# LSH attention and spatial gating on one core: from one engine in a written order to a list scheduler that orders all five

## The chip, the cores and the metric

The kernel runs on one NeuronCore of a Trainium2 chip. The metric is the device time of one execution in microseconds. The core has five engines with a queue of instructions each: PE (TensorE, matrix products), DVE (VectorE), ACT (ScalarE), POOL (GpSimd) and SP (SyncE, which issues transfers). Each works through its queue in order and waits at an instruction until what it needs is there. The three runs of the kernel before took 862.89, 864.75 and 867.11 us; the median is 864.75.

## The reference

Four batches of eight heads, 768 positions, head size 64. The attention lets a query see only keys that hash to the same bucket; the feed-forward part gates one half of its activations with a product over positions of the other half.

```python
q_bits = (np.einsum('bhsd,dk->bhsk', q, proj) > 0)      # 6 bits a row, k likewise
mask = q_bucket[:, :, :, None] == k_bucket[:, :, None, :]
scores = np.where(mask, scale * np.matmul(q, k.transpose(0, 1, 3, 2)), -1000000000.0)
attn = np.exp(scores - np.max(scores, axis=-1, keepdims=True))
attn = attn / (np.sum(attn, axis=-1, keepdims=True) + 1e-09)
x = np.matmul(attn, v)                                   # heads side by side: (4, 768, 512)

h = np.maximum(x @ w_in, 0.0)                            # 512 -> 1024
u, v = h[..., :512], h[..., 512:]
v_n = (v - mu) / np.sqrt(var + 1e-06)                    # over the 512 features
v_s = np.einsum('ts,bsd->btd', w_spatial, v_n) + b_spatial[None, :, None]
out = (u * v_s) @ w_out
```

## The kernel before, in words

**Tiling.** The 32 heads are handled as 16 pairs (four to a batch), head e = 0 and head e = 1 of a pair on the two halves of the partitions. A pair takes six steps; a step handles 128 rows of both heads against all 768 columns. fp32 numbers are split into a high and a low fp16 part, so most products are three matmuls.

**One step of a pair by queries** (all pairs but 1, 2 and 3). `scores` lets PE write two heads of scores, `sp`, with 16 matmuls (four passes; the last one, over `hk`, adds the bucket mask); DVE (L290) takes the row maximum `nb`; ACT (L291) writes the exponentials `ex`. `turn` lets ACT write the fp16 high part `pp` (L298) and DVE or POOL the low part (L299); SP issues one DMA transpose per head (L301) into `pt`. Three steps later (`LAG`) `weighted` multiplies `pt` with the split values `vp`, 18 matmuls per head, into `pv`. There are two buffers of `sp`, one per head, so the scores of the next step can't be written before the exponentials of this one have been read out.

**One step of a pair by keys** (`KEYS = {1, 2, 3}`, both heads). The scores stand with keys in the rows, so the exponentials need no transpose; they are multiplied in fp32 with `vf` (`weighted_k`, L271, six matmuls). The maxima that this needs ahead are made by `row_max` (extra matmuls `mp` and 72 DVE reductions, L242), `max_row` and `max_move`.

**Around it.** `load_qk` fetches a pair's queries and keys (one buffer, `QKB`). `hash_rows` makes the buckets' bits (PE, DVE) and moves them by eight small transfers into `hk`, from SP (pair 0: half from ACT). `split_qk` makes the fp16 parts `hl` (ACT L191, DVE L192 and L193). `normalize` (DVE, POOL, ACT) divides by the sums; `transpose_x` turns the result into `xt`. `weights_gen` fetches and converts the three weight matrices in 36 jobs. When a batch's four pairs are done, `mlp_units` makes its feed-forward part in units: `v_unit` (`vps`, six), `u_unit` (`ups`, eight), `s_unit` (`sps`, the product over positions, eight), `o_unit` (`ops`, six). `partial_units` does what can be done of the last batch without its last pair (`vpp`, `upp`).

**What sets the order.** PE's order is the order of the program (`manual_schedule(engines={ET.PE})`). In it `steps` goes through the steps; in every step `fill` hands out feed-forward matmuls by a budget of columns (`RATE`, `LRATE`), from one queue of units, a unit wholly before the next. On ACT, DVE, POOL and SP the framework's own scheduler chooses, by the priorities that `at(g, k)` sets and by its own estimate of when things are ready; so an instruction can be put ahead of others that stand earlier in the program.

Of the kernel before, what the change touches and what calls it, by code (L numbers as in the profile page):

```python
# [9 lines left out]
F16 = mybir.dt.float16  # L10
# [9 lines left out]
P = 128  # L20
# [16 lines left out]
def lsh_attention_spatial_gating(  # L37
# [22 lines left out]
    QKB = 1  # L60
    PSB = (2,2,2)
    MT = "m"
    const = ctx.enter_context(tc.tile_pool(name="const", bufs=1))
    ld = ctx.enter_context(tc.tile_pool(name="ld", bufs=2))
    wk = ctx.enter_context(tc.tile_pool(name="wk", bufs=1))
    ps_sc = ctx.enter_context(tc.tile_pool(name="ps_sc", bufs=PSB[0], space=bass.MemoryType.PSUM))
    ps_pv = ctx.enter_context(tc.tile_pool(name="ps_pv", bufs=PSB[1], space=bass.MemoryType.PSUM))
    ps_m = ctx.enter_context(tc.tile_pool(name="ps_m", bufs=PSB[2], space=bass.MemoryType.PSUM))

# [3 lines left out]
    make_identity(nc, ident)  # L73
    ones = const.tile([P, P], F32, name="ones")
    nc.gpsimd.memset(ones, 1.0)
    hc = const.tile([P, 34], F32, name="hc")
    pj, hv = hc[:, 0:32], hc[:, 32:34]

# [4 lines left out]
    for i, t in enumerate(hk):  # L83
        eng = nc.vector if i % 2 else nc.gpsimd
        eng.memset(t, 0.0)
        for e in range(2):
            eng.memset(t[D * e + 32:D * e + D, 0, :], HK)
# [5 lines left out]
    for t in vf:  # L93
        nc.gpsimd.memset(t[:, :, D:D + 1], 1.0)

# [5 lines left out]
    st = {}  # L101

    def weights_gen():
# [4 lines left out]
        jobs = []  # L108
        vi, vo, vs = (x.rearrange("(c p) f -> p c f", p=P) for x in (w_in, w_out, w_sp))
        for src, dst, n, lo, hi, m, f in ((vi, wi, NPAIR, F2, DF, 256, SX), (vi, wi, NPAIR, 0, F2, 256, SX),  # L110
                                          (vs, ws, NT, 0, S, HS, SW), (vo, wo, NF, 0, DM, 256, SX)):
            for c in range(n):
                for h in range(lo, hi, m):
                    jobs.append((src[:, c, h:h + m], [w[:, c, h:h + m] for w in dst], m, f))

        def fetch(i):
            src, _, m, _ = jobs[i]
            t = wk.tile([P, m], src.dtype, tag="raw", bufs=RB, name=f"raw{i}")
            with tc.issue_after(st["tr"]):
                nc.sync.dma_start(out=t, in_=src)  # L120
            return t

        fetched = [fetch(i) for i in range(RB - 1)]
        yield
        nc.sync.dma_start(out=bt, in_=b_sp.partition_broadcast(P))
        for i, (src, dst, m, f) in enumerate(jobs):
            raw = fetched.pop(0)
            if i + RB - 1 < len(jobs):
                fetched.append(fetch(i + RB - 1))
            if src.dtype == F32:  # L130
                w = raw
            else:
                word = raw.bitcast(U32).rearrange("p (n w) -> p w n", w=2)
                high = raw.bitcast(F32).rearrange("p (n w) -> p w n", w=2)[:, 1]
                w = wk.tile([P, m], F32, tag="wf", bufs=2, name=f"w{i}")
                wu = w.bitcast(U32)
                nc.scalar.activation(w, high, AF.Abs)
                nc.vector.tensor_scalar(w, w, TINY, None, op0=ALU.max)
                nc.vector.tensor_scalar(wu, wu, 3, 0x3FFFFFF8, op0=ALU.logical_shift_left, op1=ALU.bitwise_and)
                nc.vector.scalar_tensor_tensor(out=wu, in0=word[:, 1], scalar=0xC0000000, in1=wu, op0=ALU.bitwise_and, op1=ALU.bitwise_or)  # L140
                nc.vector.scalar_tensor_tensor(out=wu, in0=word[:, 0], scalar=29, in1=wu, op0=ALU.logical_shift_right, op1=ALU.bitwise_or)
            nc.scalar.activation(dst[0], w, AF.Copy, scale=f)
            nc.scalar.activation(w, w, AF.Copy, scale=f)
# [20 lines left out]
    def has_keys(p):  # L164
        return p in KEYS

# [541 lines left out]
```

## Time and profile before

The profiled execution took 868.83 us; its span from the first to the last instruction is 867.0 us. Busy time says how long an engine had an instruction under way, not that it worked at full rate.

| | span | busy us | instructions |
|---|---|---|---|
| PE matmul | 867.0 | 692.6 | 6622 |
| PE weight load | | 406.4 | 6622 |
| DVE | | 536.5 | 1011 |
| ACT | | 439.6 | 684 |
| POOL | | 317.7 | 320 |
| DMA, share of 16 engines, q1 | | 57.8% | 104.14 MB in all |

The mean granted clock of TensorE is 0.887. The scores of pair 0 start at 8.26 us, those of pair 4 (the first pair after the ones by keys) at 222.22 us, those of pair 15, the last one, at 741.38 us. So the program has three stretches: the beginning with pairs 0 to 3, the middle with pairs 4 to 14, beside which the feed-forward parts of three batches run, and the end with pair 15 and the last batch's feed-forward part.

### The profile page before, as it was taken

The page shows a single profiled execution, that of the slowest core. Times are in us where ns is not written, and L with a number is a line of the kernel's source. Part 1 is how long each engine was busy: PE and PEld are TensorE (multiplying, and loading weights), DVE is VectorE, ACT ScalarE, POOL GpSimd, SP SyncE. Part 2 cuts the span into 40 slices and gives each one's busy share as a digit, 9 for nine tenths or more (in the row PEclk, how much of TensorE's full clock was granted, in tenths as well). Part 3 has the DMA queues.
Part 4 walks back from the last instruction along what each step waited for, and adds up shares of the span by engine and source line. Part 5 has one row for each costly group of instructions (what it writes and reads, how often), then busy time and mean ns, then how long its engine had stood idle before and what let it go on. Part 6 is the DMA issues. An engine that isn't in the chain of part 4 may idle for free. (4 is left out here: it accounts for less than half of the span.)

```text
span 867.0 us, 16611 instructions
## 1 busy us (share of the span) xinstructions
PE 692.6 (80%) x6622; PEld 406.4 (47%) x6622; DVE 536.5 (62%) x1011; ACT 439.6 (51%) x684; POOL 317.7 (37%) x320
## 2 busy tenths in 40 slices
PE   3645569899588779697768878798879898989897
PEld 1222346577435445364434544454445464655443
DVE  5747583432657898568487959476468866672611
ACT  3324463134457576465556655565456555653511
POOL 5112242202325656318141536125322644350233
PEclk9966768799879889889779979898899899999999
DMA  4552640112357796988687765969496676874000
GB/s 131 116 146 49 165 132 19 37 41 77 65 121 184 150 208 112 190 141 163 119 164 147 133 144 107 198 115 190 89 185 133 110 139 136 150 116 103 2 37 37
DMA packets 290677, 104.14 MB, mean 120 GB/s; under 512 B 277544, under 2 KB 280616, under 8 KB 290600
## 3 DMA queue, kind: packets, MB, share of 16 engines
q1 hardware_dynamic: 290504, 103.05, 57.8%
q8 instruction: 52, 0.85, 0.4%
q14 instruction: 25, 0.20, 0.1%
q10 hardware_dynamic: 96, 0.04, 0.0%
HBM read 27.94 MB, written 6.29 MB: 39 GB/s over the span
## 5 line engine op out<-in xcount | busy, mean ns | idle before, releaser
L291 ACT ACTIVATE ex<-sp,nb 128x768 f32<-128x768 f32 x156 | 137.7, 898 | 120.4 <-DVE ex L290 120.1
L299 DVE TENSOR_TENSOR pp<-ex,pp 128x768 f16<-128x768 f32 x120 | 132.5, 1123 | 77.7 <-ACT pp L298 77.5
L230 PE MATMUL sp<-hl 64*128 64x384 f16 x1152 | 143.3, 375 | 45.7 <-ACT ex L291 43.0
L290 DVE TENSOR_SCALAR_CACHE_REDUCE ex<-sp 128x768 bf16<-128x768 f32 x156 | 142.8, 951 | 36.7 <-PE sp L230 36.4
L230 PEld LDWEIGHTS <-hl 64*128 64x128 f16 x1224 | 66.4, 104 | 153.5 <-issue 121.3
L298 ACT CAST pp<-ex 128x768 f16<-128x768 f32 x156 | 123.6, 832 | 0.1
L299 POOL TENSOR_TENSOR pp<-ex,pp 128x768 f16<-128x768 f32 x36 | 65.9, 1831 | 146.6 <-ACT pp L298 144.1
L314 PE MATMUL pv<-vp,pt 128*128 128x65 f16 x936 | 107.9, 198 | 9.2 <-DVE x L332 8.1
L478 PE MATMUL sps<-ws,vn 128*128 128x384 f16 x576 | 107.5, 336 | 6.4 <-ACT u L463 3.4
L315 PE MATMUL pv<-vp,pt 128*128 128x64 f16 x936 | 107.9, 197 | 0.0
L316 PE MATMUL pv<-vp,pt 128*128 128x65 f16 x936 | 107.6, 199 | 0.0
L314 PEld LDWEIGHTS <-pt 128*128 128x128 f16 x936 | 90.8, 101 | 32.9 <-issue 21.2
L315 PEld LDWEIGHTS <-pt 128*128 128x128 f16 x936 | 90.2, 100 | 13.0 <-issue 1.6
L316 PEld LDWEIGHTS <-pt 128*128 128x128 f16 x936 | 90.5, 100 | 0.0
L496 PE MATMUL ops<-wo,g 128*128 128x512 f16 x288 | 74.7, 398 | 19.6 <-ACT g L484 12.4
L333 POOL TENSOR_TENSOR x<-x,xf 128x384 f32<-128x384 f32 x31 | 36.2, 1168 | 124.9 <-DVE x L332 120.7
L478 PEld LDWEIGHTS <-vn 128*128 128x128 f16 x576 | 54.0, 100 | 50.2 <-issue 15.6
L456 PE MATMUL ups<-xt,wi 128*128 128x384 f16 x348 | 66.6, 336 | 5.5 <-ACT u L463 4.4
L271 PE MATMUL pv<-vf,ex 128*128 128x65 f32 x432 | 60.6, 299 | 6.9 <-DVE x L332 6.9
L230 PE MATMUL sp<-hk 63*128 63x384 f16 (+1 forms) x384 | 60.6, 366 | 4.8 <-DMA hk<-sg 4.8
L271 PEld LDWEIGHTS pv<-vf,ex 128*128 128x128 f32 x432 | 56.8, 213 | 15.2 <-issue 15.1
L483 POOL TENSOR_TENSOR sy<-sy,u 128x384 f32<-128x384 f32 x32 | 35.5, 1108 | 73.2 <-DVE sy L482 65.0
(95 smaller groups left out, 971.5 us busy)
## 6 DMA issues: line engine op xcount, KB each, us to landing
qk<-kq SPq DMA_DIRECT2D x16, 768.0 KB
out<-o SPq DMA_DIRECT2D x24, 256.0 KB
v<-v SPq DMA_DIRECT2D x13, 384.0 KB
raw<-w_in SPq DMA_DIRECT2D x16, 256.0 KB
pt<-pp SPq DMA_TRANSPOSE x156
raw<-w_sp SPq DMA_DIRECT2D x12, 192.0 KB
raw<-w_out SPq DMA_DIRECT2D x8, 256.0 KB
hk<-sg SPq DMA_DIRECT2D x124, 9.0 KB
```

What stands on the lines that cost most here:

```text
L230: nc.tensor.matmul(ps[e][:, c - halves[0]], lhsT=f(l)[:, rows], rhs=f(m)[:, cs], start=(a == 0), stop=(a == len(passes) - 1))
L271: nc.tensor.matmul(acc[:, qi, :], lhsT=ex[:, qi * P:(qi + 1) * P], rhs=vf[p % 2][:, 2 * i + e, :], start=(i == 0 and qi == 0), stop=(i == ...
L290: nc.vector.tensor_scalar(jk, ps[e], -ISQ, None, op0=ALU.mult, op1=ALU.min, accum_out=nb)
L291: nc.scalar.activation(ex, ps[e], AF.Exp, bias=nb, scale=ISQ)
L298: nc.scalar.copy(pp[:, 0], ex)
L299: (nc.gpsimd if (e, i) in (PL_POOL if n >= 2 * NH else PL_POOL1) else nc.vector).tensor_tensor(out=pp[:, 1], in0=ex, in1=pp[:, 0], op=ALU. ...
L314: nc.tensor.matmul(acc, lhsT=pt[:, c, :], rhs=vh, start=(i == 0 and c == 0), stop=False)
L315: nc.tensor.matmul(acc[:, 0:D], lhsT=pt[:, c, :], rhs=vl, start=False, stop=False)
L316: nc.tensor.matmul(acc, lhsT=pt[:, NT + c, :], rhs=vh, start=False, stop=(i == NT - 1 and c == NT - 1))
L456: nc.tensor.matmul(ps[:, :HS], lhsT=wi[gw][:, c, d * P:(d + 1) * P], rhs=xt[c][:, gx, hs], start=(k == k0), stop=(k == 3 * NPAIR - 1))
L478: nc.tensor.matmul(ps[:, :HS], lhsT=vn[gv][:, c, d * P:(d + 1) * P], rhs=ws[gw][:, c, hs], start=(k == 0), stop=(k == 3 * NT - 1))
L496: nc.tensor.matmul(ps, lhsT=gt[h][gg][:, c, j * P:(j + 1) * P], rhs=wo[gw][:, c, :], start=(k == 0), stop=(k == 3 * NF - 1))
```

## The change

The kernel is written anew around a planner, and the arithmetic stays. Every piece of work is an `op` with an engine, an assumed duration, the ops it waits for, the buffers it holds and a rank. `timetable` plays the program through once while the kernel is built: on the engine that can start first it takes, of all that is ready, the one of lowest rank. The ops are then issued in the order of their planned starts, on all engines (`manual_schedule()` without a list). What the plan assumes is used for the order alone: on the chip each engine works through its queue as before.

Beside that:

- `KEYS` now names heads, {2, 4, 6}: pairs 1 to 3 have head 0 by keys and head 1 by queries. There are 174 transposes of `pt` (156 before), 72 matmuls of row maxima (144), 36 reductions (72), 108 fp32 weightings (216) and 3132 in fp16 (2808).
- The bits of pairs 1 to 15 are moved by transfers that POOL issues (`HQ_REST`), 120 of them; SP issues four moves, ACT four.
- Feed-forward sums are cut into groups of three matmuls, each an op of its own that is ranked behind the attention; units whose inputs are ready may overtake others.
- POOL makes the low part `pp` of head 1 in all steps of pairs 0 to 3, in three of six steps of pairs 4 to 7, in two of six from pair 8 on. Before it had four of six up to pair 7 and two of six after.
- Buffers: `ex` 3 (4), `pp` 3 (4), `pt` 6 (7), `v32m` 6 (4), `u` 2 (1), the queries and keys of pair 1 in a `u` buffer.

The order on ACT, at the split of pair 10's queries and keys (`hl10`), before. `ex14`, `ex15` and `pp14`, `pp15` are the two heads of pair 7, steps 4 and 5:

```order
L298 CAST pp14_4_4318<-ex14_4_4312 128x768
L298 CAST pp15_4_4323<-ex15_4_4315 128x768
L484 CAST g0_0_1_3989<-sy0_2_1_4329 128x384
L191 ACTIVATE hl10_4778<-qk10_4285 128x1536
L291 ACTIVATE ex14_5_4408<-sp7_5_0_4390,nb14_3878 128x768
L291 ACTIVATE ex15_5_4411<-sp7_5_1_4391,nb15_3882 128x768
L298 CAST pp14_5_4414<-ex14_5_4408 128x768
```

The same split now. `ex16` and `ex17` are the heads of pair 8, steps 1 and 2:

```order
L447 ACTIVATE ex16_1_4638<-sp8_1_0_4591,nb16_4565 128x768
L447 ACTIVATE ex17_1_4663<-sp8_1_1_4592,nb17_4578 128x768
L828 ACTIVATE o0_0_4680<-ops0_0_4574 128x512
L451 CAST pp16_1_4706<-ex16_1_4638 128x768
L451 CAST pp17_1_4712<-ex17_1_4663 128x768
L339 ACTIVATE hl10_4735<-qk10_4401 128x1536
L447 ACTIVATE ex16_2_4756<-sp8_2_0_4686,nb16_4565 128x768
```

The split has moved from the last step of pair 7 to behind the exponentials of step 1 of pair 8. On SP the load of `qk10` keeps its place behind the transposes of step 3 of pair 7.

The order on SP at the beginning, before. `hk1` and `hk2` are the buckets of pairs 1 and 2, `pt0` and `pt1` the heads of pair 0:

```order
L151 DMA qk2_198<-kq 128x1536
L301 DMA_TRANSPOSE pt0_0_168<-pp0_0_165 128x12x128
L301 DMA_TRANSPOSE pt1_0_173<-pp1_0_170 128x12x128
L184 DMA hk1_83<-sg1_1_184 12x384 x8
L301 DMA_TRANSPOSE pt0_1_228<-pp0_1_225 128x12x128
L301 DMA_TRANSPOSE pt1_1_233<-pp1_1_230 128x12x128
L184 DMA hk2_84<-sg1_2_242 12x384 x8
L301 DMA_TRANSPOSE pt0_2_284<-pp0_2_281 128x12x128
```

The same moves now, on POOL, among its shares of `pp`:

```order
L328 DMA hk1_76<-sg1_1_156 12x384 x8
L456 TENSOR_TENSOR pp1_0_217<-ex1_0_191,pp1_0_217 128x768
L328 DMA hk2_77<-sg1_2_246 12x384 x3
L456 TENSOR_TENSOR pp1_1_275<-ex1_1_233,pp1_1_275 128x768
L328 DMA hk2_77<-sg1_2_246 12x384 x4
L456 TENSOR_TENSOR pp1_2_368<-ex1_2_327,pp1_2_368 128x768
L328 DMA hk2_77<-sg1_2_246 12x384
```

Eight moves per pair have left SP's queue, where they stood between transposes, and stand in POOL's, between pieces of `pp`.

The order on PE where the first product over positions of the third batch begins (`sps2_0_0`; the 2 is the batch), before; this stands between steps 4 and 5 of pair 13:

```order
L456 MATMUL ups2_3_0_8079<-xt11_7270,wi0_102 128x384
L456 LDWEIGHTS wi1_103
L456 MATMUL ups2_3_0_8079<-xt11_7270,wi1_103 128x384
L478 LDWEIGHTS vn2_0_7272
L478 MATMUL sps2_0_0_8113<-ws0_104,vn2_0_7272 128x384
```

The same product now, behind the last weighting of pair 15 (`pv31`, `pt31_5`):

```order
L544 MATMUL pv31_9037<-vp1_88,pt31_5_9383 128x64
L545 LDWEIGHTS pt31_5_9383
L545 MATMUL pv31_9037<-vp1_88,pt31_5_9383 128x65
L620 LDWEIGHTS vn2_0_8945
L620 MATMUL sps2_0_0_9451<-ws0_102,vn2_0_8945 128x384
```

From the first scores of pair 15 on PE has 108 `ops`, 216 `sps`, 73 `ups`, 18 `vps`, 54 `vpp` and 36 `upp` matmuls before; now 144, 288, 156, 42, 54 and 36.

The diff, cut to its core:

```diff
-    with tc.manual_schedule(engines={ET.PE}):
-        steps()
+    timetable(free, banks)
+    with tc.manual_schedule():
+        for o in sorted(ops, key=lambda o: o.start):
+            o.fn()
...
-    KEYS = {1, 2, 3}
+    KEYS = {2, 4, 6}
+    keys = lambda p: [e for e in range(2) if 2 * p + e in KEYS]
+    byq = lambda p: [e for e in range(2) if 2 * p + e not in KEYS]
...
+    def timetable(free, banks):
...
+            t0, e = best
+            pick = None
+            for o in came[e]:
+                r = o.ready
...
+                if r <= t0 + LOOK:
+                    rank = o.rank if isinstance(o.rank, tuple) else (step[0] + (4 if o.rank > 8 else 0), o.rank)
+                    if pick is None or rank < pick[0]:
+                        pick = (rank, o, max(r, t0))
+            _, o, t = pick
+            came[e].remove(o)
+            o.start, end = t, t + o.d
+            free[e] = end
...
+            for a in o.then:
+                a.ready = max(a.ready, end + o.land + (0.0 if a.e == o.e and not o.land else X))
+                a.left -= 1
+                if not a.left:
+                    came[a.e].append(a)
...
-                HQS[(2 * j + e) % len(HQS) if p < 1 else 0].dma_start(
+                q, eng = HQ_FIRST[e] if p == 0 else HQ_REST
+                at["hk", p].append(op(q, 0.75, move, t, on=[g1, k], rank=3, land=2.0))
...
-        nc.scalar.activation(hl[:, 1:3], qk, AF.Copy, scale=SQ)
+        t = op("A", 1.42, high, at["qk", p], *after, on=[qk, h], rank=4)
...
+        t = op("P", 1.5, go, *at["hl", p], *at["hk", p], on=[sc, held["hl", p], held["hk", p]], rank=(g, 0))
+        t.ready = begin
+        for e in range(2):
+            (by_keys if 2 * p + e in KEYS else by_queries)(p, i, e, g, t, sc)
...
+        t = op("V", 0.92, low, t, on=[sc, hx, held["nb", n]], rank=(g, 0.1 + 0.1 * e))
+        t = op("A", 0.87, exp, t, on=[sc, hx], rank=(g, 0.1 + 0.1 * e))
+        t = op("A", 0.77, half, t, on=[hx, hp], rank=(g, 1 + e))
+        t = op("G" if gp else "V", 1.8 if gp else 0.95, rest, t, on=[hx, hp], rank=(g, 1 + e))
+        at["pt", n, i] = op("S", 1.4, turn, t, on=[hp, ht], rank=(g, 1 + e), land=2.4)
...
+        for k in range(0, len(products), 3):
...
+            t = op("P", 3 * COST[width], go, t, *(list(after) + [a for h in into for a in h.before] if k == 0 else ()), on=on,
+                   rank=9 + 1e-4 * len(ops), need=(pool, 1) if k == 0 else None)
...
-    RATE = 7000
-    LRATE = 8200
+    POOL0 = tuple((1, i) for i in range(NT))
+    POOL1 = ((1, 0), (1, 2), (1, 4))
+    POOL2 = ((1, 1), (1, 4))
+    EB, PB, PTB, XTB, VB, UB = 3, 3, 6, 6, 6, 2
+    LAG, LAG0, LAGK = 3, 2, 2
+    T_FIRST, T_KEYS, T_QUERIES, T_LAST = 5.0, 4.8, 5.8, 5.8
+    LOOK = 0.2
+    HQ_FIRST = (("S", nc.sync), ("A", nc.scalar))
+    HQ_REST = ("G", nc.gpsimd)
+            if i == 1 and p + 2 < NP:
+                hash_rows(p + 2, now)
+            if i == 2 and p + 2 < NP:
+                split_qk(p + 2, now)
+            if i == 3 and p + 3 < NP:
+                load_qk(p + 3, now)
```

1052 lines of the change are left out of this document (587 added, 465 removed).

## The prediction

> **What bounds the kernel now.** I read the page first, then the windows by stage, the waits, and one pair's timeline.
>
> ```profile
> span 867.0 us, 16611 instructions
> PE 692.6 (80%) x6622; PEld 406.4 (47%) x6622; DVE 536.5 (62%) x1011; ACT 439.6 (51%) x684; POOL 317.7 (37%) x320
> ```
>
> PE looks like the bound, but its busy time is stretched wherever its clock is below 1.00. The windows cut the span at the first scores of pairs 0, 4 and 15:
>
> ```profile
> 0.00:17.00 17.00, 4.57 (x23) 1.30 (x24) 7.22 (x8) 4.36 (x4) 11.16 (x21) 1.00 0.55 167
> 17.00:222.00 205.00, 152.21 (x1194) 96.91 (x1193) 110.31 (x246) 81.62 (x134) 45.37 (x56) 0.80 0.33 83
> 222.00:741.00 519.00, 422.27 (x4483) 244.93 (x4481) 367.33 (x654) 303.40 (x461) 219.69 (x203) 0.89 0.74 145
> 741.00:867.00 126.00, 113.60 (x932) 63.30 (x928) 51.63 (x105) 50.19 (x87) 41.51 (x40) 0.99 0.35 71
> 300.00:350.00 50.00, 41.73 (x473) 25.34 (x471) 46.18 (x82) 32.82 (x58) 33.01 (x31) 0.91 0.76 155
> 350.00:400.00 50.00, 40.55 (x445) 24.59 (x444) 31.43 (x55) 28.68 (x41) 18.28 (x18) 0.90 0.85 158
> ```
>
> Columns are window, length, then busy time of PE, PEld, DVE, ACT and POOL with counts, clock, DMA share and GB/s. In the first two rows, 222 us, no engine is near full: PE 152 of 205 at clock 0.80, DVE 0.54. The middle, 519 us, is 47.2 us a pair; DVE is 0.71 busy there, yet 0.92 in the fifth row. Only in the end is PE full, at full clock. So the first two stretches wait more than they work. On what, one pair shows:
>
> ```profile
> 404.51 1.01 SPq L151 DMA_DIRECT2D qk<-kq  x1
> 405.64 5.14 SPq L301 DMA_TRANSPOSE pt<-pp  x2
> 410.04 1.48 ACT L191 ACTIVATE hl<-qk 128x1536 f16<-128x1536 f32 x1 [4.74 <-DMA qk<-kq]
> 411.43 1.68 ACT L291 ACTIVATE ex<-sp,nb 128x768 f32<-128x768 f32 x2
> 415.02 1.03 PE L496 MATMUL ops<-wo,g 128*128 128x512 f16 x2 [6.58 <-ACT g L484]
> ```
>
> The split of a later pair stands on ACT in front of this step's exponentials and waits 4.74 us for a load issued just before; the exponentials, whose end frees the score banks, and the feed-forward copy queue behind it, and PE idles 6.58 us. It recurs:
>
> ```profile
> ACT hl L191 <- DMA qk<-kq: 43.8, 10, 6.7
> ACT ex L291 <- DVE ex L290: 120.1, 51, 5.9
> 26.77 6.12 SPq L184 DMA_DIRECT2D hk<-sg  x8
> 53.03 0.94 PE L230 MATMUL mp<-hl 64*128 64x384 f16 x2 [10.81 <-DVE mx L242]
> ```
>
> The first row has ten such waits, 43.8 us. The last two are the beginning: eight small moves hold SP 6.12 us between transposes, and PE stands 10.81 us in one place, its reductions queued on DVE behind weight work.
>
> **The beginning, priced by its busiest engine.** With half the heads of pairs 1 to 3 by queries POOL gets more work than DVE. Rows:
>
> ```profile
> L299 POOL TENSOR_TENSOR pp<-ex,pp 128x768 f16<-128x768 f32 x36 | 65.9, 1831 | 146.6 <-ACT pp L298 144.1 <-PE sp L230 2.2
> L325 POOL TENSOR_TENSOR xf<-fm,fl 128x384 f32<-128x384 f32 x32 | 33.3, 1042 | 2.0
> L333 POOL TENSOR_TENSOR x<-x,xf 128x384 f32<-128x384 f32 x31 | 36.2, 1168 | 124.9 <-DVE x L332 120.7
> L207 POOL TENSOR_TENSOR va<-v 128x384 f32<-128x384 f32 x13 | 16.8, 1293 | 1.0
> L144 POOL TENSOR_TENSOR wi<-w,wi 128x256 f16<-128x256 f32 x16 | 11.4, 715 | 44.1 <-ACT w L143 44.1
> L184 SPq DMA_DIRECT2D hk<-sg x124: 713/714/1388, 12.5 to 674.8; - x124
> ```
>
> By the order POOL has in pairs 0 to 3: 24 `pp` at 1.83 (43.9 us); 24 weight parts, 16 at 0.71 and 8 of 384 columns near 1.02 (19.5); five means of v, 1.29 and two smaller adds, 2.5 in all (12.4); six `fl` and `xf` at 1.33 (8.0); six `x` at 1.17 (7.0). That is 90.8 us. To it come 40 moves (pairs 1 to 5). POOL issues no transfer before, so their price is bounded: 0.71 us, SP's minimum in the last row, if POOL issues as fast; 2.6 us if each also stands behind the longest DVE `pp` (1.906 us, the row below). I take 1.0, close to the row of the same transfer: 131 us. DVE's share is less: 30 row maxima, 6 `pp`, 36 reductions instead of 72, 16 weight jobs, splits and sums make 119 us after 17 us by the group means. The 17 us ahead of the first scores' mask stay, since pair 0's moves stay on SP and ACT.
>
> An engine fed by others is not full. I take 0.87 for its share: above the 0.79 that the middle would have if only the 43.8 us of `hl` went (376 / 475, the 376 from below), near the 0.92 of the best window, because the moves, the other stall of SP, go as well. Beginning: 17 + 131 / 0.87 = 168 us, from 222.
>
> **The middle, priced by DVE.** The largest groups:
>
> ```profile
> L290 DVE TENSOR_SCALAR_CACHE_REDUCE ex<-sp 128x768 bf16<-128x768 f32 x156 | 142.8, 951 | 36.7 <-PE sp L230 36.4
> L299 DVE TENSOR_TENSOR pp<-ex,pp 128x768 f16<-128x768 f32 x120 | 132.5, 1123 | 77.7 <-ACT pp L298 77.5
> L290 DVE TENSOR_SCALAR_CACHE_REDUCE ex<-sp x156: 923/952/959, 17.4 to 777.9; 128x768 bf16<-128x768 f32 x156
> L339 DVE TENSOR_TENSOR xs<-x,xs 128x384 f16<-128x384 f32 x32 | 29.3, 918 | 10.4 <-ACT xs L338 10.3
> L299 DVE TENSOR_TENSOR pp<-ex,pp x120: 926/959/1906, 21.4 to 781.8; 128x768 f16<-128x768 f32 x120
> L299 POOL TENSOR_TENSOR pp<-ex,pp x36: 1633/1682/2762, 21.7 to 775.6; 128x768 f16<-128x768 f32 x36
> ```
>
> For pairs 4 to 14 the order has 132 maxima (busy per instruction 142.8 / 156 = 0.915: 120.8 us), 105 `pp` (132.5 / 120 = 1.104: 115.9) and 22 `xs` (20.1). The remaining splits, sums, hashes, statistics and 8 weight jobs make 119 at their group means: 376 us, as good as the 367 that stand in the window before. DVE's work does not shrink; the gaps should. At 0.87 the middle is 376 / 0.87 = 432 us (39.3 a pair); at 0.92 it is 409, at 0.79 476, at today's 0.71 530. PE must fit in: 333 us at full clock by the rows below for what the order leaves in these pairs (66 score groups, 130 weightings, 192 `vps`, 192 `ups`, 288 `sps`, 144 `ops`). It would bind only at a clock under 0.77 (half rate 46% of the time). The 132 transposes are the same as before; the 18 extra ones stand in pairs 1 to 3, where the DMA share is 0.33.
>
> **The end, priced by PE.** What left the middle is paid here. Spacings at clock 1.00:
>
> ```profile
> 741.45 1.41 PE sp L230 x16
> 732.08 0.19 PE L314 MATMUL pv<-vp,pt 128*128 128x65 f16 x1
> 732.60 0.20 PE L316 MATMUL pv<-vp,pt 128*128 128x65 f16 x1
> 795.23 1.94 PE vpp L365 x9
> 797.17 5.85 PE upp L365 x36
> 803.02 1.96 PE vps L404 x9
> 810.24 7.97 PE ups L456 x48
> 820.95 3.43 POOL vn L437 x3
> 842.43 11.71 PE sps L478 x72
> 857.46 5.58 PE ops L496 x25
> ```
>
> A weighting is 18 matmuls from 732.08 to 732.60, 0.031 us each. From pair 15 on the order has 96 `sp` (8.5 us), 288 `pv` (8.9), 42 `vps` (9.1), 156 `ups` (25.9), 288 `sps` (46.8), 54 `vpp` (11.7), 36 `upp` (5.9), 144 `ops` (32.1): 149 us. Of these 53 us are the last batch's own chain, which before runs from 803.02 to 867 in 64 us, gaps such as the 3.43 us on POOL included, and whose order is unchanged. So 96 + 64 = 160 us, against 126.
>
> **Small edits.** Fewer `ex`, `pp` and `pt` buffers cost nothing while DVE sets the pace, since three `ex` cover a step and the next head; without that cover a step would wait for the `pp` of the head before, up to 1.1 us. Row maxima that take one bank instead of two, earlier memsets and two `u` buffers lie beside other work. Fewer fp32 weightings and more fp16 ones are PE work in pairs 1 to 3, where PE has room.
>
> **Sum.** 168 + 432 + 160 = 760 us of span. The profiled run is 868.83 against a span of 867.0, and the median 864.75 is 0.9953 of it: (760 + 1.8) x 0.9953 = 758 us.
>
> **Rivals.**
>
> 1. *The queues stay full.* At 0.92 in both stretches and 0.71 us a move: 17 + 119 / 0.92 = 147, 409, 157: 713 of span, 711 us. For it: a window of before does it for 50 us. Against: POOL and DVE hold each other up (POOL's `pp` from 1633 to 2762 ns), and one late op holds a whole queue.
> 2. *Transfers or gaps hold the middle.* The DMA share there is 0.74 x 519 = 384 us, which in 432 would be 0.89, above the 0.85 of the sixth window. At 0.85 the middle is 452; with only the `hl` waits gone it is 476, and a beginning at 0.79 is 183: 780 to 819 of span, 778 to 817 us. For it: transposes still run in order on SP. Against: three steps lie between a transpose and its use.
> 3. *POOL's moves become the bound: slower.* POOL has 19 us a pair in pairs 4 to 13 (185 by the same rows) and eight moves. At 0.87 POOL passes DVE's 39.3 from 1.9 us a move. At 2.4 the beginning is 17 + 187 / 0.87 = 232 and a pair 43.9: 760 + 64 + 46 = 870, the tie. At the upper bound, 2.6, it is 241 and 45.7: 760 + 73 + 64 = 897 of span, 895 us. For it: the minimum and maximum of both `pp` rows show the two engines waiting for each other. Against: the maxima that read PSUM (L290 stays within 923 to 959 ns) show no such wait.
> 4. *The plan is no better than the order it replaces.* DVE stays at 0.71 and POOL reaches no more: 17 + 131 / 0.71 = 201, 530, 160: 891 of span, 888 us, slower, since the end has grown by 34. Against: the `hl` wait can't recur, as six transposes of two steps stand between a load and its split.
>
> On rival 3 the Trainium skill is sharper: "SBUF — State Buffer", section "SBUF: two separate sides", says that descriptors of a GpSimd transfer can't be written while VectorE holds the shared port; its section "A bandwidth-pool intuition that's wrong (but worth ruling out)" has about 3.1 us instead of 0.62 for one. At 3.1 a move the beginning would be 264 and a pair 50.3, 966 of span. The two `pp` rows agree that the engines exclude each other; no run here yet shows a transfer from POOL.
>
> **Chances.** Forecast (735 to 780) 0.47; rival 1 0.20; rival 2 0.17; rival 3 0.08; rival 4 0.05; some mixture that ends even 0.03. A difference of 0.5%, 4 us, is about what can be told from none. Faster is 0.47 + 0.20 + 0.17 less 0.01 for rival 2's upper tail, 0.83; same 0.04; slower 0.13. The range: down to 702, a little under rival 1's 711; up to 838, past rival 2's 817, leaving most of rivals 3 and 4 out.
>
> **What would show it.** First scores of pair 4 near 168 and of pair 15 near 600; pairs of 39 us, DVE near 0.87 busy there; no wait of ACT `hl` for `qk`; the stretch after pair 15 near 160 with PE full. POOL's moves near 1 us, and the beginning bound by POOL. I'd be wrong if pairs stay at 45 us, if POOL's moves pass 2 us, or if the clock in the middle falls under 0.77.

## The result, and the profile after

The changed kernel takes 761.07 us (median of 4 runs, 757.79 to 766.26), beside 865.93 us before (4 runs, 862.89 to 867.13). The ratio is 0.8799, 95% interval 0.8743 to 0.8855. The profiled execution took 757.79 us; its span is 756.0 us and its mean clock 0.935.

The page of the changed kernel, the span and the engines:

```profile
span 756.0 us, 16947 instructions
PE 637.4 (84%) x6655; PEld 372.6 (49%) x6655; DVE 556.8 (74%) x1007; ACT 460.6 (61%) x705; POOL 413.7 (55%) x453
```

The windows of the changed kernel, with the columns as before. The rows end at 17 us and at the first scores of pair 4 and of pair 15; the fifth row is the stretch that was the best one before, the last one the sixth step of pair 0:

```profile
0.00:17.00 17.00, 6.28 (x34) 2.05 (x35) 12.10 (x18) 5.67 (x6) 10.83 (x25) 0.98 0.60 188
17.00:162.50 145.50, 116.28 (x1201) 77.65 (x1200) 115.98 (x226) 95.11 (x158) 91.59 (x104) 0.83 0.77 160
162.50:592.00 429.50, 363.66 (x4317) 210.88 (x4316) 364.48 (x636) 296.54 (x432) 252.92 (x269) 0.95 0.91 174
592.00:756.00 164.00, 151.15 (x1105) 82.04 (x1104) 64.25 (x128) 63.28 (x113) 58.34 (x55) 0.99 0.28 61
300.00:350.00 50.00, 39.80 (x457) 22.61 (x454) 42.25 (x64) 30.25 (x41) 30.73 (x34) 0.93 0.94 181
38.80:58.80 20.00, 10.98 (x137) 7.98 (x135) 15.51 (x33) 8.67 (x18) 7.70 (x8) 0.62 1.05 225
```

The three stretches are 162.5, 429.5 and 164.0 us, where before they were 222, 519 and 126. The middle does almost the same DVE work as before (364 us beside 367) in 89 us less time; the DMA share there has risen from 0.74 to 0.91. The end is longer by 38 us, since more feed-forward work has been left to it.

The waits of the changed kernel (total us, times, longest):

```profile
POOL pp L456 <- ACT pp L451: 100.1, 25, 13.0
ACT ex L447 <- DVE ex L444: 97.3, 69, 3.4
...
PEld L543 <- DMA pt<-pp: 74.6, 52, 4.6
...
PE pv L543 <- DMA pt<-pp: 58.0, 39, 4.1
...
ACT pp L451 <- DMA pt<-pp: 23.7, 25, 3.3
...
ACT hl L339 <- DMA qk<-kq: 3.7, 1, 3.7
```

The split's wait for its load has gone from 43.8 us to 3.7. In its place there is a wait that was hardly there before: PE's matmuls wait for transposes 39 times and its weight loads 52 times. The kernel before had one such wait, by the view of the line that transposes (L301, who waited for it):

```profile
  PEld L314: 0.2, 1
```

The line that moves the bits of the buckets, in the changed kernel: its row of the page (busy us and mean ns, then POOL's idle time before it), then its own view (ns, minimum, median and maximum; then the time to landing):

```profile
L328 POOL DMA_DIRECT2D hk<-sg x120 | 64.8, 545 | 39.9 <-issue 28.5
```

```profile
L328 POOL DMA_DIRECT2D hk<-sg x120: 521/521/749, 12.4 to 552.0; - x120
...
DMA to landing us min/median/max: 1.6/3.4/6.2
```

And the transposes' issue on SP, by the view of their line:

```profile
L460 SPq DMA_TRANSPOSE pt<-pp x174: 1306/1560/4432, 20.0 to 629.7; - x174
```

### The profile page after: what moved, and what is told of

Same layout as the page of the kernel before. It is cut to its first block, busy times and chain, and to the rows that moved or that the text cites. A ratio compares the mean times of both kernels' runs of the same rounds, so it can differ in the third digit from the quotient of the medians.

```text
span 756.0 us, 16947 instructions
## 1 busy us (share of the span) xinstructions
PE 637.4 (84%) x6655; PEld 372.6 (49%) x6655; DVE 556.8 (74%) x1007; ACT 460.6 (61%) x705; POOL 413.7 (55%) x453
## 5 line engine op out<-in xcount | busy, mean ns | idle before, releaser
L447 ACT ACTIVATE ex<-sp,nb 128x768 f32<-128x768 f32 x174 | 154.9, 900 | 99.4 <-DVE ex L444 97.3
L444 DVE TENSOR_SCALAR_CACHE_REDUCE ex<-sp 128x768 bf16<-128x768 f32 x174 | 160.3, 951 | 30.5 <-PE sp L416 30.4
L543 PE MATMUL pv<-vp,pt 128*128 128x65 f16 x1044 | 118.5, 199 | 65.5 <-DMA pt<-pp 58.0
L451 ACT CAST pp<-ex 128x768 f16<-128x768 f32 x174 | 140.6, 829 | 24.4 <-DMA pt<-pp 23.7
L543 PEld LDWEIGHTS <-pt 128*128 128x128 f16 x1044 | 99.4, 101 | 108.3 <-DMA pt<-pp 74.6
L456 POOL TENSOR_TENSOR pp<-ex,pp 128x768 f16<-128x768 f32 x52 | 91.2, 1753 | 101.6 <-ACT pp L451 100.1
L544 PE MATMUL pv<-vp,pt 128*128 128x64 f16 x1044 | 117.6, 198 | 0.0
L545 PE MATMUL pv<-vp,pt 128*128 128x65 f16 x1044 | 117.2, 199 | 0.0
L544 PEld LDWEIGHTS <-pt 128*128 128x128 f16 x1044 | 100.7, 100 | 2.5 <-issue 1.4
L545 PEld LDWEIGHTS <-pt 128*128 128x128 f16 x1044 | 101.0, 101 | 0.0
L328 POOL DMA_DIRECT2D hk<-sg x120 | 64.8, 545 | 39.9 <-issue 28.5
L801 DVE SCALAR_TENSOR_TENSOR sy<-sps,bt 128x384 f32<-128x384 f32 x32 | 17.8, 555 | 71.4 <-PE sps L620 71.4
L620 PE MATMUL vps<-wi,xt 128*128 128x512 f16 x234 | 56.7, 385 | 0.0
```

What stands on the lines that cost most here:

```text
L328: eng.dma_start(out=hk[p % NHK][D * e:D * e + 2 * NB, 1 - j // 2, (j % 2) * HS:(j % 2 + 1) * HS], in_=sg[1][32 * j + 16 * e:32 * j + 16 * ...
L444: nc.vector.tensor_scalar(jk, st["sc", p, i][e], -ISQ, None, op0=ALU.mult, op1=ALU.min, accum_out=st["nb", n][:, i:i + 1])
L447: nc.scalar.activation(st["e32", n, i], st["sc", p, i][e], AF.Exp, bias=st["nb", n][:, i:i + 1], scale=ISQ)
L451: nc.scalar.copy(st["pp", n, i][:, 0], st["e32", n, i])
L456: eng.tensor_tensor(out=st["pp", n, i][:, 1], in0=st.pop(("e32", n, i)), in1=st["pp", n, i][:, 0], op=ALU.subtract)
L543: nc.tensor.matmul(acc, lhsT=pt[:, c, :], rhs=vh, start=(i == 0 and c == 0), stop=False)
```

## The experiments

Three questions are open behind a time that came out as forecast. Is the middle really set by DVE, as the forecast's price had it, or by the transposes for which PE now waits? Is the beginning really set by POOL? And which part of the rewrite carries the gain: the order of the queues, the moves, the mix of heads, or the feed-forward sums that overtake? Stage times below come from one profiled execution each, medians from four runs or more.

### What paces the middle: half the transposed bytes, a lighter DVE, both

Half the transposed bytes:

```diff
-            nc.sync.dma_start_transpose(out=st["pt", n, i], in_=st.pop(("pp", n, i)).rearrange("p g c k -> p (g c k)"))
+            nc.sync.dma_start_transpose(out=st["pt", n, i][:, 0:NT], in_=st.pop(("pp", n, i))[:, 0].rearrange("p c k -> p (c k)"))
...
-                nc.tensor.matmul(acc, lhsT=pt[:, NT + c, :], rhs=vh, start=False, stop=(i == NT - 1 and c == NT - 1))
+                nc.tensor.matmul(acc, lhsT=pt[:, c, :], rhs=vh, start=False, stop=(i == NT - 1 and c == NT - 1))
```

> The changed kernel, but each transpose of the exponentials turns only the high half (six blocks instead of twelve); the third matmul of a weighting uses the high half again, so the low half of the exponentials is left out of the result. Work on PE, DVE, ACT and POOL stays. Theory A (DVE paces the middle, as the prediction has it): the middle stays within 2% of its 430 us and the median within 1.5% of 761 us. Theory B (the transposes pace it: DMA share 0.91 there, PE waits 58 us for pt): the middle drops by at least 30 us, the beginning by about 10, median 715 to 725 us.

A lighter `pp` on DVE (both inputs are fp16, so that an instruction took 0.559 us instead of 0.958, by the medians; it writes zeros):

```diff
-            eng.tensor_tensor(out=st["pp", n, i][:, 1], in0=st.pop(("e32", n, i)), in1=st["pp", n, i][:, 0], op=ALU.subtract)
+            ex = st.pop(("e32", n, i))
+            eng.tensor_tensor(out=st["pp", n, i][:, 1], in0=ex if gp else st["pp", n, i][:, 0], in1=st["pp", n, i][:, 0], op=ALU.subtract)
```

> The changed kernel, but DVE's share of the pp low part subtracts the fp16 high part from itself, so it writes zeros (the low half of these exponentials is left out); with two fp16 inputs it should take about half of its 0.96 us. Transposes stay. Theory A (DVE paces the middle): 105 instructions save about 0.6 us each, the middle drops by 40 to 70 us, median 700 to 725 us. Theory B (transposes pace it): the middle stays within 2%, median 750 to 765 us.

Both edits together:

> Both edits together (half transposes and the short pp on DVE; the low half of the exponentials is left out). Theory A: no faster than the run with the short pp alone. Theory B: no faster than the run with half transposes alone. If both pace the middle in turn, it is faster than either by more than 15 us; then the PE's 333 us of work set the next floor, middle 360 to 380 us, median 690 to 710 us.

Measured: half the bytes 737.83 us (ratio to the kernel before 0.8536, 0.8499 to 0.8572), the lighter DVE 744.6 us (0.8601, 0.857 to 0.8633), both 717.06 us (0.8287, 0.8254 to 0.8319). No median lies in a range that its expectation gave; that both edits would be faster than either by more than 15 us held (21 and 28). The middle with half the bytes, from the windows:

```profile
160.70:569.70 409.00, 357.71 (x4319) 210.28 (x4318) 366.37 (x636) 294.61 (x432) 252.61 (x269) 0.96 0.60 120
```

With the lighter DVE:

```profile
164.50:581.10 416.60, 357.76 (x4317) 207.20 (x4316) 320.17 (x636) 296.11 (x432) 232.83 (x269) 0.96 0.96 180
```

With both:

```profile
162.00:557.10 395.10, 355.74 (x4317) 209.08 (x4316) 325.16 (x636) 293.92 (x432) 231.79 (x269) 0.95 0.63 124
```

From 429.5 us, half the bytes take 20.5, the lighter DVE 12.9, both 34.4: the two savings add up (33.4). The medians of the whole time say the same, with 23, 16 and 44 us. If the slower of two had set the pace alone, one of the single edits would have brought nothing and the other all. So DVE does not set the pace alone: of the 44 us of DVE work that the second edit takes away, 12.9 arrive in the time.

What the first edit took away is not the bytes alone. A transpose of both halves can't go before DVE or POOL has written the low half; a transpose of the high half alone can. SP's longest wait at the transposes, over the whole of the changed kernel:

```profile
SPq L460 <- DVE pp L456: 126.5, 74, 7.0
```

With half the bytes, where DVE's `pp` no longer stands among the waits of the transposes, it is for ACT's cast:

```profile
SPq L460 <- ACT pp L451: 104.8, 42, 7.0
```

So the edit makes the transposes smaller and lets them start earlier, and these runs do not tell the two apart; a part of the 20.5 us may be DVE's. Since the lighter DVE brings 13.9 us (409.0 to 395.1) where the transposes no longer wait for it, and 12.9 where they do, most of its gain likely comes through what stands behind `pp` in DVE's own queue.

PE's waits for `pt` after pair 4 starts are 39.5 us in the changed kernel and 18.6 with half the bytes; with the lighter DVE they stay at 40.2. The row of the changed kernel, from the waits between 165 and 570 us:

```profile
PE pv L543 <- DMA pt<-pp: 39.5, 24, 4.1
```

The same row with half the bytes:

```profile
PE pv L543 <- DMA pt<-pp: 18.6, 9, 3.9
```

And with the lighter DVE:

```profile
PE pv L544 <- DMA pt<-pp: 40.2, 30, 4.4
```

With both edits PE is busy for 355.74 of 395.10 us, 0.90. Even then the middle is not at the 333 us of PE work that the prediction counted.

### What paces the beginning: more POOL work, less DVE work

More work behind each move on POOL:

```diff
+    pad = const.tile([P, 90], F16, name="pad")
...
                     eng.dma_start(
                         out=hk[p % NHK][D * e:D * e + 2 * NB, 1 - j // 2, (j % 2) * HS:(j % 2 + 1) * HS],
                         in_=sg[1][32 * j + 16 * e:32 * j + 16 * e + 2 * NB, :])
+                    if 1 <= p <= 5:
+                        for _ in range(3):
+                            nc.gpsimd.memset(pad, 0.0)
```

> The changed kernel with three small memsets of a spare tile on POOL (128x90 fp16, some 0.17 us each by the rows of POOL's other memsets, 0.5 us together) behind each of the 40 moves of pairs 1 to 5; nothing else is added, and all orders stay. A move then takes POOL about 1.05 us, which is the price that the prediction took. Theory A (the prediction's step: POOL is the bound of the beginning): 32 of them lie ahead of pair 4, 17 us more of POOL there, and the first scores of pair 4 go from 162.5 to 178 to 184; 775 to 783 us. Rival B (POOL is 0.63 busy there and has room; the beginning is paced by another engine): first scores of pair 4 within 6 us of 162.5, 757 to 768 us.

Less work for DVE in the weight jobs:

```diff
-                t = op("V", 0.25, lambda c=c: nc.vector.tensor_scalar(c["w"], c["w"], TINY, None, op0=ALU.max), t, on=hold, rank=R_W)
+                t = op("V", 0.25, lambda: None, t, on=hold, rank=R_W)
...
(likewise the three lines that follow)
```

> The changed kernel without the four DVE instructions of each weight job that rebuild a weight from its 64 bits (the weights are then only the magnitude of their upper words); the plan is made as if they were there, so that all orders stay. 16 of the 24 jobs lie in the beginning, where the four lines are 7.0 + 9.5 + 14.9 + 8.6 = 40 of DVE's 116 us. Theory A (DVE paces the beginning, 0.80 busy): first scores of pair 4 from 162.5 to 125 to 140, 735 to 752 us in all. Rival B (DVE and the transposes take turns there, as e1 to e3 showed of the middle): half of it or less, first scores of pair 4 at 143 to 155. Rival C (POOL paces the beginning, as the prediction had it): within 5 us of 162.5.

Measured: 764.06 us (0.8788, 0.8747 to 0.8829) with more POOL work, 755.34 us (0.8694, 0.8641 to 0.8746) with less DVE work. Both intervals overlap with that of the changed kernel. The beginning with more POOL work, from the windows:

```profile
17.00:167.00 150.00, 117.76 (x1201) 78.85 (x1200) 110.30 (x226) 95.24 (x158) 109.62 (x217) 0.84 0.76 156
```

With less DVE work:

```profile
17.00:157.90 140.90, 112.52 (x1201) 77.10 (x1200) 79.78 (x162) 95.09 (x158) 89.38 (x104) 0.82 0.79 165
```

18 us more of POOL work (109.62 beside 91.59) cost 4.5 us. 36 us less of DVE work (79.78 beside 115.98) brought 4.6. Executions of the changed kernel differ by 8 us among themselves, so neither is clear of noise. Each of the three rivals is off: POOL alone is not the bound, DVE alone is not, and with half the transposed bytes pair 4 starts at 160.7, 1.8 us earlier, so the transposes alone are not either. What is left untested is that two of them hold it in turn, so that only an edit of both would help. For it: without the weights' bits DVE waits longer for scores, and PE for transposes. The waits of the beginning, in the changed kernel:

```profile
PE pv L543 <- DMA pt<-pp: 15.6, 11, 4.0
DVE ex L444 <- PE sp L416: 14.3, 10, 2.9
```

With less DVE work:

```profile
DVE ex L441 <- PE sp L413: 34.3, 16, 6.7
...
PE pv L540 <- DMA pt<-pp: 23.6, 12, 4.6
```

What the beginning waits for is not settled by these runs. What stays the same in all of them is PE's share: 116.28 of 145.50 us, 117.76 of 150.00, 112.52 of 140.90, that is 0.80, 0.79 and 0.80, at a clock of 0.82 to 0.84. That fits a chain that goes through PE again and again at a lowered clock; it was not tested.

One place can be seen. The sixth step of pair 0 takes 20 us (38.80 to 58.80, the last row of the windows above), with the DMA share at 1.05 (a share above 1 says that this figure is not exact) and the clock at 0.62. SP's queue there:

```profile
40.99 2.95 SPq L460 DMA_TRANSPOSE pt<-pp  x1
43.99 0.57 SPq L228 DMA_DIRECT2D bt<-b_sp  x1
44.66 6.17 SPq L460 DMA_TRANSPOSE pt<-pp  x3
50.89 1.38 SPq L235 DMA_DIRECT2D raw<-w_in  x2
```

The issues of the three transposes that start at 44.66, from the view of their line between 44 and 51 us:

```profile
L460 SPq DMA_TRANSPOSE pt<-pp x3: 1413/1438/1468, 44.7 to 49.4; - x3
```

Loads of weights and the spread `b_sp` go in among the transposes. The first transpose shown takes SP 2.95 us to issue, where the median of all is 1.56. The three that follow take up to 1.47 us each; the rest of their 6.17 us SP waits between them. With fewer bytes transposed the step is still 16.6 us long; what keeps it long is not shown.

### Which part of the change carries the gain

**Only PE by the plan.** The other four queues take the order that the framework's scheduler gives them, as before:

```diff
-    with tc.manual_schedule():
+    with tc.manual_schedule(engines={ET.PE}):
```

> The scheduler of the changed kernel sets PE's order alone; DVE, ACT, POOL and SP take their instructions as the program's own priorities give them, in which the split of a later pair again stands ahead of the last exponentials of its step on ACT. Theory A (what the plan gained was gained on the queues of ACT, DVE and SP, by no late instruction standing ahead of others): the middle back to 470 to 519 us, 810 to 865 us in all. Rival B (the order of PE's work, with the mix and the moves on POOL, carries the gain, and the other queues follow it): 762 to 790 us.

Measured: 822.99 us, ratio 0.9506 (0.9456 to 0.9557); 62 us above the changed kernel. The windows:

```profile
11.00:209.60 198.60, 136.89 (x1220) 88.92 (x1221) 130.72 (x267) 112.83 (x192) 116.75 (x133) 0.77 0.62 137
209.60:656.90 447.30, 374.02 (x4318) 219.99 (x4318) 336.94 (x606) 280.32 (x398) 231.68 (x250) 0.93 0.85 159
656.90:825.00 168.10, 154.11 (x1105) 84.52 (x1104) 61.37 (x125) 62.80 (x112) 56.24 (x54) 0.97 0.26 58
```

The two profiled executions differ by 69 us: 47 of them are lost in the beginning, 18 in the middle, 4 at the end. So the order of the four queues is worth most where weight jobs, maxima and exponentials of four pairs meet; a piece of ACT's timeline shows it, with weight jobs (`ws`, `wi`) ahead of the exponentials in the last row:

```profile
86.36 0.52 ACT L264 ACTIVATE ws<-raw 128x384 f16<-128x384 f32 x1 [0.50 <-DMA raw<-w_sp]
86.79 0.40 ACT L264 ACTIVATE wi<-w 128x256 f16<-128x256 f32 x1
...
87.83 0.88 ACT L447 ACTIVATE ex<-sp,nb 128x768 f32<-128x768 f32 x1
```

In the middle, most of the gain is there without the plan for those four: 447.3 us, where it was 519 before. The expectation had the split's wait come back; it did not (ACT waits 4.3 us for it in this run), so this run does not price it. Each theory is right in part: the total lies in the range of the first, but the middle, for which it gave 470 to 519, came out lower, since PE's order carries a part of the gain, as the second has it.

**The waits of the split, alone.** In the kernel before, a column of the split is first written from this step's exponentials, so that the split can't stand ahead of them:

```diff
+        if hold is not None:
+            nc.scalar.copy(hl[:, 1, 0:1], hold)
         nc.scalar.activation(hl[:, 1:3], qk, AF.Copy, scale=SQ)
...
-            split_qk(p + 2)
+            split_qk(p + 2, st.get("last"))
```

> The kernel before, with one edit: a copy of one column makes the split of the queries and keys (hl) on ACT depend on the current step's pp, so it can't be put ahead of an earlier step's exponentials. Prediction's reading: the ten waits of hl for its load (43.8 us in all) go, and most of them were on the path: 820 to 835 us. Rival (the waits only shift to another place): within 1% of 866 us.

Measured: 833.97 us, ratio 0.9634 (0.9592 to 0.9677). The middle, from 519:

```profile
218.00:709.00 491.00, 411.96 (x4484) 240.97 (x4484) 368.34 (x655) 307.82 (x472) 224.59 (x203) 0.92 0.79 153
```

One late instruction that stood ahead of others cost about 32 us of the 105. The prediction's sum for its removal alone, 476 us in the middle, was 15 us too good: the waits were 43.8 us, of which 3.7 are left in this run, and the middle got 28 us shorter.

**The moves.** Back on SP in the changed kernel, and alone on POOL in the kernel before:

```diff
-    HQ_REST = ("G", nc.gpsimd)
+    HQ_REST = ("S", nc.sync)
...
(the kernel before)
-                HQS[(2 * j + e) % len(HQS) if p < 1 else 0].dma_start(
+                (HQS[(2 * j + e) % len(HQS)] if p < 1 else nc.gpsimd).dma_start(
```

> The 112 moves of hash bits that the changed kernel issues from POOL are issued from SP again, as before the change; the plan knows of it and orders all queues anew. Theory A (the prediction's: the moves were a stall of SP, whose row of before shows eight of them holding the transposes for 6.12 us): about 0.71 us of SP a move, 5.7 us a pair in front of transposes of which two or three steps are under way; the middle gets 10 to 30 us longer, 770 to 795 us. Rival B (three steps lie between a transpose and its use, so where the moves are issued does not matter once the plan sets their places): 755 to 767 us. Rival C (moves on POOL cost more than on SP, since POOL adds, too, and its slow pp are waited for): faster than the changed kernel, 745 to 755 us.

> The kernel before, with the hash bits of pairs 1 and later moved from POOL's queue instead of SP's; nothing else. Theory A (the moves on SP, 6.12 us for eight of them, held the transposes and through them the whole pair): 3 to 6 us a pair, the middle from 519 to 455 to 490, 800 to 835 us. Rival B (three steps lie between a transpose and its use and cover them; in the changed kernel the same edit backwards cost some 9 us): 845 to 868 us. Rival C (in an order that was not made for it the moves stand behind slow adds on POOL and come late): above 870 us.

Measured: back on SP 770.18 us (0.8905, 0.8837 to 0.8973), which overlaps with the changed kernel's interval at its edge; alone on POOL 869.06 us (1.002, 0.9988 to 1.0053), no change. Middle and end with the moves back on SP:

```profile
164.10:618.00 453.90, 378.63 (x4392) 218.11 (x4393) 369.17 (x650) 298.36 (x436) 209.45 (x182) 0.95 0.87 166
618.00:769.00 151.00, 139.90 (x1048) 76.78 (x1047) 58.90 (x115) 59.75 (x105) 58.09 (x56) 1.00 0.30 65
```

The middle of the kernel before with the moves on POOL:

```profile
216.10:740.10 524.00, 425.96 (x4482) 245.21 (x4481) 381.23 (x655) 304.73 (x461) 257.75 (x283) 0.89 0.75 144
```

Its moves, by the view of their line:

```profile
L184 POOL DMA_DIRECT2D hk<-sg x120: 518/518/864, 24.4 to 671.6; - x120
```

In the first, time and middle lie within the ranges of its first theory (770 to 795 us, 10 to 30 us longer). But the plan has also drawn some feed-forward work from the end into the middle (1048 matmuls are left, not 1105), so that 13 of the 24 us lost in the middle come back at the end. In the second SP no longer issues the eight moves that held it for 6.12 us, and the time does not move. So where these transfers are issued is worth nothing by itself in the order before, and some 9 us at most in the planned one, where the plan changes with it.

**The mix.** Both heads of pairs 1 to 3 by keys again:

```diff
-    KEYS = {2, 4, 6}
+    KEYS = {2, 3, 4, 5, 6, 7}
```

> Pairs 1 to 3 have both heads by keys again, as before the change; the scheduler and all else stay. Theory A (the mix takes 36 key-sided reductions off DVE in the beginning, and pp that POOL can share come in their place; the beginning is then paced by DVE): first scores of pair 4 from 162.5 to 180 to 200 us, the rest within 5 us, 778 to 800 us. Rival B (the plan made the whole gain of the beginning, and the mix only trades one work for another): first scores of pair 4 at 155 to 168, 753 to 768 us.

**No overtaking.** Each feed-forward sum is chained to the one before it:

```diff
+    chain = [None]
...
-        t = None
+        t = chain[0]
...
+        chain[0] = t
```

> The feed-forward sums are chained, each after the one before it, as the order of before had them; the scheduler and the mix stay. Theory A (sums that overtake give PE work while one of them waits for its gate or its copy, and without it PE stands): middle and end together 10 to 25 us longer, 770 to 786 us. Rival B (PE has room in the middle, 364 busy of 429.5 us, and the end is a chain of sums that wait for the last pair in any order): 756 to 766 us.

Measured: 771.23 us (0.8907, 0.8869 to 0.8945) without the mix, 767.41 us (0.8859, 0.882 to 0.8897) without overtaking. The beginning without the mix from 17 us on, as in the other tables, and the end:

```profile
17.00:189.40 172.40, 136.28 (x1182) 89.19 (x1181) 120.47 (x267) 93.09 (x171) 79.64 (x106) 0.78 0.49 117
...
617.40:771.00 153.60, 142.62 (x1054) 76.99 (x1053) 60.26 (x115) 58.87 (x103) 54.01 (x52) 0.98 0.31 63
```

Middle and end without overtaking:

```profile
160.80:587.30 426.50, 357.48 (x4268) 208.03 (x4267) 357.22 (x630) 295.17 (x429) 249.96 (x269) 0.93 0.91 174
587.30:763.70 176.40, 164.46 (x1156) 87.40 (x1155) 65.11 (x135) 65.19 (x116) 56.10 (x55) 0.98 0.26 59
```

The mix takes 27 us off the beginning (189.4 to 162.5), as its theory had it. The reason that the theory gave, reductions off DVE, is the smaller part: from 17 us on DVE has 4.5 us less work (115.98 beside 120.47) and PE 20 us less busy time (116.28 beside 136.28, at clocks of 0.83 and 0.78). PE's share is 0.79 without the mix, too. 10 of the 27 us are paid at the end, where 1105 matmuls are left instead of 1054, and the medians differ by 10 us; the intervals don't overlap. The 51 matmuls that overtaking takes out of the end (1156 to 1105) are worth 12.4 us there, and the middle and the beginning are 4.7 us longer for it; the medians differ by 6 us, and the intervals overlap, so a small gain is likely and not certain.

### Four `pp` buffers again

```diff
-    EB, PB, PTB, XTB, VB, UB = 3, 3, 6, 6, 6, 2
+    EB, PB, PTB, XTB, VB, UB = 3, 4, 6, 6, 4, 2
```

> The changed kernel with four pp buffers, as before the change, instead of three, and four buffers for the fp32 rows of v instead of six, since they must share the room; the plan knows of both. Theory A (fewer pp buffers cost nothing, as the prediction said, since something else sets the pace): 755 to 767 us. Rival B (ACT's 25 waits for a transpose to free a pp buffer, 23.7 us, lie on the path): 740 to 752 us. Rival C (fewer rows of v hold the end's chain): slower, 768 us or more, with the loss behind the first scores of pair 15.

Measured: 777.41 us, ratio 0.8931 (0.8883 to 0.8978), slower than the changed kernel. Middle and end:

```profile
165.60:598.50 432.90, 359.13 (x4262) 211.22 (x4261) 366.60 (x629) 291.61 (x427) 245.79 (x269) 0.92 0.90 171
598.50:777.80 179.30, 166.41 (x1162) 88.36 (x1161) 62.96 (x135) 66.37 (x118) 55.38 (x56) 0.98 0.27 61
```

ACT's 25 waits for a transpose to free a `pp` buffer are gone, and nothing was gained: the middle is 3.4 us longer. 15 us are lost at the end, where 1162 matmuls are left instead of 1105, as the third theory has it. Since `pp` and the rows of v changed in one run, which of them made the plan leave more to the end stays open. None of the versions that compute the whole reference beat the changed kernel.

## Why the prediction was right, and where by luck

The forecast of 758 us stands beside 761.07 measured, and the three stretches of its sum, 168, 432 and 160, beside 162.5, 429.5 and 164.0. Not all of it was right for the reason given.

**The beginning** came out within 6 us by a step that was wrong, so by luck. "The beginning, priced by its busiest engine" took POOL for that engine. A move takes 0.545 us of POOL on average (64.8 us for 120), not 1.0, below even the lower bound of 0.71 that came from SP's row; POOL's work after 17 us is 91.6 us, not 131: 17.1 are moves, for which the prediction had 40, and 74.5 the rest, for which it had 90.8. Its share is 0.63, not 0.87, and the two errors cancel. When each move was brought to the price assumed (0.52 us and three memsets of 0.174), the beginning went up by 4.5 us, not by the 17 that a bound by POOL gives. DVE, at 0.80, is no bound either. That a stretch of four pairs has an engine that can be divided by a share of 0.87 was the failed step; which chain sets it is open. The time that the mix takes off the beginning, 27 us, is there, but only 4.5 us of work left DVE with it.

**The middle** was priced by DVE at 376 / 0.87 = 432. The work is 364.5 us, the share 0.85, the stretch 429.5. The price was good; the reading that DVE sets the pace was half of it, so that the number is in part luck. DVE's 44 us less gave 12.9, the transposes of the high half alone 20.5, and the two add up. So something of rival 2 is there as well, though not its time: the prediction held against it that three steps lie between a transpose and its use, and PE waited 58.0 us for transposes all the same. The DMA share went to 0.91, past the 0.85 that rival 2 took for the most it would reach, and to 0.96 with a lighter DVE. The step that failed is this cover. Three steps of the middle took 23.6 us on average before and 19.5 now; whether the transposes come late by what they take or by when they start is open. Where PE waited long, DVE can be behind it. In pair 9 a step goes from 376.62 to 387.11 us, and shortly before its end PE waits 3.28 us for a transpose. The window of that step:

```profile
376.62:387.11 10.49, 7.21 (x91) 4.05 (x89) 10.49 (x13) 6.53 (x11) 10.17 (x13) 1.00 0.80 126
```

SP's queue there, then the issues of these three transposes and SP's longest wait, both from views of 373 to 383 us:

```profile
373.68 9.19 SPq L460 DMA_TRANSPOSE pt<-pp  x3
...
L460 SPq DMA_TRANSPOSE pt<-pp x3: 1439/1447/1847, 373.7 to 381.0; - x3
...
SPq L460 <- DVE pp L456: 6.8, 2, 3.4
```

DVE is busy for the whole of that step, and POOL for 10.17 us of it. Of the 9.19 us in which SP issues three transposes, each takes at most 1.85 us; most of the rest is the second of SP's two waits for a low half from DVE, 3.4 us. So in this step DVE is full, as the prediction had it, and the transposes are late behind it.

**The waits of `hl`** went, as forecast: 43.8 us to 3.7. Alone they were worth 32 us in the time. The eight moves between SP's transposes, which the prediction named as "the other stall of SP" in choosing its share of 0.87, were worth nothing in the old order.

**The end** was priced by PE's spacings: 149 us of work and 160 us in all; the window has 151 and 164.0. This part was right step by step, and so was "PE must fit in", at a clock of 0.95 and 0.85 busy in the middle.

**Rival 1** (0.92 and 711 us) was off: DVE's share in the middle is 0.85 and not 0.92, and PE, DVE and the transposes wait for each other there, as the waits show. **Rival 3** fell by its price: the longest issue of a move was 0.749 us, where the tie needed 2.4. The prediction took a figure of the Trainium skill, "SBUF — State Buffer", section "A bandwidth-pool intuition that's wrong (but worth ruling out)", 3.1 us instead of 0.62 for one transfer beside a DVE operation, as the time for which a move holds POOL. That is not seen here: beside a DVE that is 0.80 busy in the beginning and 0.85 in the middle, 120 moves held POOL for 0.521 to 0.749 us each. They landed after 1.6 to 6.2 us, so that a wait inside the transfer is not excluded; it did not lengthen the issue. POOL also stood idle for 39.9 us ahead of the moves, 28.5 of them for nothing that the profile shows. **Rival 4** fell, and only PE's order by the plan gives 823 us: the queues of the other four engines needed it too.

**Small edits** were costed at nothing. Fewer fp32 weightings were held to be PE work where PE has room; the run without the mix fits this badly, since 27 us of the beginning went with 20 us of PE's busy time. Four `pp` buffers instead of three gained nothing, which agrees; that the version as a whole lost 16 us shows that such an edit changes the plan, and through it what is left for the end.

## What to carry to other kernels

A sum of an engine's work over a share can give the right time for a stretch that this engine does not set; before building on it, take work off that engine and see how much of it arrives in the time, since here 36 us off DVE brought 4.6 in one stretch and 44 brought 12.9 in another. Look in the trace at what else an edit sets free: transposing half the bytes also let the transposes go ahead of DVE's low halves, and so it can't say what the bytes cost. When one wait is removed, ask which transfer was covered by it: the transposes that hardly anything waited for became 58 us of waits on PE once the steps were shorter. Where a planner sets the order of all queues, an edit of one buffer or queue moves work between stretches, so stage times say more about the edit than the total.

## What the hardware showed that was not expected

- A small transfer (12 rows of 768 bytes) issued from POOL holds it for 0.521 us, less than the 0.714 us that the same transfer holds SP (medians), and beside a DVE that is 0.80 to 0.85 busy never more than 0.749 us (0.864 in the old order).
- A transpose's issue on SP has a median of 1.56 us and a maximum of 4.43 us. With half the bytes, where the DMA share of the middle is 0.60 instead of 0.91, the view of the same line has 1.217 and 2.239 us. That the long issues come from full DMA engines is likely, but not shown, since these transposes are smaller as well.
- The DMA share goes to 0.96 over 417 us with the lighter DVE, and to 1.05 in a 20 us stretch, so the 0.85 in the sixth window of the kernel before was no limit; the share above 1 also says that the figure is not exact.
